# Batch 0 in high and low parts: weights decoded by ScalarE and an integer add, norms by reciprocal root

## The chip, the cores and the metric

The kernel runs on one core of a Trainium2 chip. The metric is device time in microseconds (us), the median of several runs; smaller is better. TensorE is the matrix engine (PE in the rows, PEld its weight loads), VectorE the elementwise engine (DVE), ScalarE the activation engine (ACT), GpSimd (POOL) and SyncE (SP) issue transfers.

## The reference

A linear attention (batch 8, 8 heads, 576 rows, 64 per head), normed per head, feeds a gated layer with a product over the rows:

```python
kv  = einsum('bhsd,bhse->bhde', k, v);  out = einsum('bhsd,bhde->bhse', q, kv)
x   = out / sqrt(mean(out*out, -1) + 1e-6) * g_norm          # then heads side by side: (8, 576, 512)
h   = maximum(x @ w_in, 0);  u, v = h[..., :512], h[..., 512:]
v_n = (v - mean(v)) / sqrt(var(v) + 1e-6)
v_s = einsum('ts,bsd->btd', w_spatial, v_n) + b_spatial[None, :, None]
return (u * v_s) @ w_out
```

All inputs are float32, and the host hands the two weight matrices over as int64 words, the pairs of which are float32 bits of two neighbouring columns seen as one double; the kernel decodes them.

## The kernel before, in words

**Numbers in two parts.** From batch 1 on every large product is made of three: a float32 number is cut in a high part (a cast to the matrix engine's rounded type `F32R`) and a low part (the rest), and high x high, high x low and low x high are summed in the accumulator (`hl`, L319; `three`, L313). A cut is a pair: ScalarE casts the high part, VectorE subtracts it from the number (`split`, L353 and L354; `split_w`, L727 and L728; `split_x`, L258 and L259). Batch 0 is made otherwise: its products take plain float32 (`hv_32`, L404; `hv_tail_32`, L410; `u_32`, L428; `sp_32`, L437 and L438), so that the first products need no cut. Its operands lie in `X32`, `W32`, `V32`, `VT32`. The weights are cut later, for batch 1, by `split_in` (token X) and `split_ws` (token E).

**Decoding.** A tile of 128 rows of a weight matrix (512 KB as int64 words) is decoded by one ScalarE step (`weight64_a`, L713) and five VectorE steps (`weight64_b`, L719 to L723). There are 12 such tiles, 8 of `w_in` in the first 45 us, 4 of `w_out` up to batch 1.

**Norms.** A reciprocal root (`rsqrt_a`, `rsqrt_b`) is a square root on ScalarE (L199) beside a product and a reciprocal on VectorE (L200, L201), and three small VectorE steps that correct it (L206 to L208). One is made for each pair of heads and each 128 rows of `v`.

**Order.** For batch 0 the string `PLAN` (L35) is a list of tokens: W and L start loads, c and C decode a weight, J and K make K^T V, A and D the attention rows and their squares, B their norm, T the transpose and the copy of `x`, H the product for v (chunk c, part k), e, F relu and norm of v, u the product for u, h the tail rows, s a spatial product with the gate. For batches 1 to 7 the strings `SEVEN`, `GATED`, `FIRST`, `EVEN`, `ODD` order the seven products of each 2x2 scheme, the steps of the next batch's attention and the output products. What the tokens emit is then put in order on each engine by the framework's scheduler, within the brackets and bars of the plan in program order. Engines run their queues in order.

**Memory.** `vpool` holds two tiles of 14 x 256 columns: for batch 0 they are `X32`, `W32`, `VT32`, from batch 1 on `VH` and `VL`. `WSH`, `WSL` hold seven quadrants of the cut spatial weights, `ps_mm` four accumulator banks, which H, u and s use in turn.

Of the kernel before, what the change touches and what calls it, by code (L numbers as in the profile page):

```python
# [8 lines left out]
F32 = mybir.dt.float32  # L9
# [37 lines left out]
p11 p61 p10 p20 p60 p21 p50 p70 p40 p51 p71 p41 p30 p31  # L47
# [3 lines left out]
p50 p10 p60 p70 p11 p20 p61 p40 p21 p30 p51 p71 p41 p31  # L51
# [3 lines left out]
p p p s p s s s s p p s p p p w s p p p s p p o o s o s o s s w s o s  # L55
# [3 lines left out]
s v v v s v s u y s s u s u u u u s u u s u u s s u u s u u s p p p s s s s p s s p p p p s p p s p  # L59
p s s p p s o o o o s s  # L60
# [3 lines left out]
v v v v u u u u u u s u s u u u u u u s u p p s s p p p p p s p p s s p s p p s s s s s p p o s o s  # L64
o o s o
# [8 lines left out]
def body(ctx: ExitStack, tc, qT, kvm, kvt, g2, w_in, wsT, bsp, w_out, out):  # L74
# [34 lines left out]
    VH = VL = None  # L109
    R = [vpool.tile([P, 14 * HF], F32, name=f"R{x}", tag=f"V{x}") for x in "HL"]  # L110
    X32 = R[0][:, 0:NP * XC].rearrange("p (k t) -> p k t", t=XC)
    VT32 = R[0][:, NP * XC:NP * XC + FH]
    W32 = [R[1][:, n * FH:(n + 1) * FH] for n in range(7)] + [R[0][:, NP * XC + FH:]]
# [82 lines left out]
    def rsqrt_a(ss, n, rows, mul, tag):  # L196
        a, s0, q, r = (small.tile([P, n], F32, name=f"{x}{tag}", tag=f"{x}{tag}")[0:rows]
                       for x in "asqr")
# [3 lines left out]
        return s0, q, r  # L202
# [58 lines left out]
    def att_t(b, p, st):  # L261
        x = st[p]
        ps = ps_att.tile([P, 512], F32, name="pstr", tag="att")
        for c in range(NC):
            nc.tensor.transpose(ps[:, c * P:(c + 1) * P], x[:, c * P:(c + 1) * P], ident)  # L265
        if b == 0:
            nc.scalar.activation(X32[:, p, 0:NT], ps, AF.Copy, scale=gcol)
        else:
            split_x(ps, XH[:, p, 0:NT], XL[:, p, 0:NT])

    def att_tail(b, st):
# [6 lines left out]
        if b < 2:  # L278
            nc.scalar.activation(X32[:, :, cols], v, AF.Copy, scale=gcol)
            cols = slice(TAILC[0], TAILC[0] + TAIL)  # L280
        if b == 0:
            return
        split_x(v, XH[:, :, cols], XL[:, :, cols])
# [101 lines left out]
    def hv_tail():  # L385
# [3 lines left out]
                   hl(XH[:, k, cols], XL[:, k, cols], WVH[:, k], WVL[:, k])])  # L389
# [13 lines left out]
    def hv_32(c, k):  # L403
        nc.tensor.matmul(psv[c], X32[:, k, c * P:(c + 1) * P], W32[k], start=k == 0,  # L404
                         stop=k == NP - 1)

    def hv_tail_32():
# [632 lines left out]
```

## Time and profile before

| | |
|---|---|
| median of 3 runs | 513.22 us (512.23 to 513.38) |
| span of the profiled execution | 511.2 us |
| around the span, median less span | 2.0 us |
| TensorE / its weight loads | 498.9 us (98%) / 438.4 us (86%) |
| VectorE | 408.8 us (80%) |
| ScalarE | 292.8 us (57%) |
| matrix instructions | 3436 |
| transfers | 72.22 MB, mean 141 GB/s |
| table loads on ScalarE | 1, of 1.283 us |

A profile is one execution. Its own time is known by its span alone, from the first to the last instruction; what the timed runs have beyond it lies around the program. A float32 product appears as two matrix instructions in a row, a product of high or low parts as one. Matrix instructions overlap, so one's duration is not what it costs in a row of them: a row's length by its count is.

### The profile page before, as it was taken

To read this page: it belongs to the slowest core of one execution; us is meant where nothing else is said; L and a number is where in the kernel's file an instruction comes from. 1 tells how busy PE (TensorE), PEld (TensorE's weight loads), DVE (VectorE), ACT (ScalarE), POOL (GpSimd) and SP (SyncE) were. 2 spreads that over 40 slices of the span, in tenths; PEclk is the share of its full clock that TensorE was granted. 3 is DMA by queue.
4 is the path that set the end of the run, shared out by engine and by line. 5 is a ranking of instruction groups with operands and counts; after the bars stand their busy time and mean duration, and the time that the engine had idled before them with its cause. 6 is when DMAs were issued, how large, how long until landed. Compare 5 with 4: busy or idle time off the path is not lost.

```text
span 511.2 us, 9846 instructions
## 1 busy us (share of the span) xinstructions
PE 498.9 (98%) x3436; PEld 438.4 (86%) x3436; DVE 408.8 (80%) x1193; ACT 292.8 (57%) x1000; POOL 28.7 (6%) x58
## 2 busy tenths in 40 slices
PE   6999999999999999999999999999999999999996
PEld 6758788898888899989998899988998889988995
DVE  3898599688997889778795689878898589987870
ACT  2555456896734796456641689347742579536421
POOL 5000000000010300010000100010000100010000
PEclk9999999999999999999999999999999999999999
DMA  7995300635354435354426615324444512315213
GB/s 256 311 347 193 103 23 2 238 90 174 123 193 137 129 126 207 117 170 138 133 93 228 203 41 194 112 78 176 135 165 144 171 30 63 131 42 165 91 76 103
DMA packets 28293, 72.22 MB, mean 141 GB/s; under 512 B 3602, under 2 KB 8210, under 8 KB 26708
## 3 DMA queue, kind: packets, MB, share of 16 engines
q1 hardware_dynamic: 23412, 48.01, 28.6%
q0 software_dynamic: 4832, 23.60, 13.9%
q8 instruction: 27, 0.44, 0.4%
q14 instruction: 22, 0.18, 0.1%
HBM read 58.48 MB, written 13.11 MB: 140 GB/s over the span
## 4 chain that ended last, share of the span: by engine, by line
PE 78%; DVE 8%; ACT 7%; DMA 5%; issue 1%; SPq 0%; ACTq 0%; DVEq 0%
PE pso L317 15%; PE psh L350 12%; PE psb L566 7%; PE pso L237 4%; PE psc L566 4%; PE psa L566 4%; PE psub L566 4%; PE pskv L162 4%; PE psu L428 3%; PE psa L437 3%; PE psua L566 3%; PE psh L404 3%; PE psuc L566 2%; PE pstr L265 2%; DMA KV<-kvm 2%; ACT x L220 2%
## 5 line engine op out<-in xcount | busy, mean ns | idle before, releaser
L317 PE MATMUL pso<-WO,G 128*128 128x512 f32 x384 | 94.4, 397 | 0.0
L317 PEld LDWEIGHTS pso<-WO,G 128*128 128x128 f32 x384 | 70.6, 188 | 14.5
L353 ACT CAST G<-SUMg 128x288 fp32r<-128x288 f32 (+1 forms) x56 | 22.8, 406 | 44.6 <-DVE SUMg L588 44.4
L220 ACT ACTIVATE x<-pso 128x64 f32<-128x64 f32 x208 | 44.8, 254 | 5.7 <-PE pso L237 5.5
L220 ACT ACTIVATION_READ_ACCUMULATOR x<-pso 128x1 f32 x208 | 43.9, 240 | 0.0
L350 PE MATMUL psh<-WVL,XH 128*128 128x512 f32 x112 | 43.9, 392 | 0.0
L350 PE MATMUL psh<-WVH,XH 128*128 128x512 f32 x112 | 43.8, 396 | 0.0
L350 PE MATMUL psh<-WVH,XL 128*128 128x512 f32 x112 | 43.3, 391 | 0.0
L668 ACT COPY o<-pso 128x512 f32<-128x512 f32 x35 | 20.2, 594 | 38.9 <-PE pso L317 28.7
L354 DVE TENSOR_TENSOR VL<-v,VH 128x512 fp32r<-128x512 f32 (+1 forms) x56 | 34.6, 620 | 2.7 <-ACT VH L353 2.2
L353 ACT CAST VH<-v 128x512 fp32r<-128x512 f32 (+1 forms) x56 | 31.7, 574 | 3.3 <-DVE v L382 2.1
L337 ACT ACTIVATE v<-v,mv,rv 128x512 f32<-128x512 f32 x28 | 23.5, 840 | 10.6 <-DVE mv L336 10.5
L354 DVE TENSOR_TENSOR G<-SUMg,G 128x288 fp32r<-128x288 f32 (+1 forms) x56 | 23.4, 417 | 7.2 <-ACT G L353 6.9
L258 ACT ACTIVATE XH<-pstr,gcol 128x512 fp32r<-128x512 f32 x28 | 19.4, 700 | 11.4 <-PE pstr L265 11.2
L566 PE MATMUL psb<-WSH,VH 128*128 128x288 f32 x84 | 25.6, 305 | 0.3 <-DVE U L549 0.2
L329 DVE BATCH_NORM_STATS2 s<-v 128x6 f32<-128x512 f32 x32 | 21.9, 689 | 4.5 <-ACT v L323 3.9
L350 PEld LDWEIGHTS psh<-WVH,XH 128*128 128x128 f32 x112 | 21.0, 188 | 4.6 <-ACT o L668 0.2
L350 PEld LDWEIGHTS psh<-WVL,XH 128*128 128x128 f32 x112 | 21.1, 188 | 4.4
L566 PE MATMUL psb<-WSL,VH 128*128 128x288 f32 x84 | 24.8, 295 | 0.0
L350 PEld LDWEIGHTS psh<-WVH,XL 128*128 128x128 f32 x112 | 21.0, 188 | 4.3
L162 PEld LDWEIGHTS pskv<-KV 128*64 128x64 f32 x512 | 18.1, 140 | 7.8 <-issue 3.9
L566 PE MATMUL psb<-WSH,VL 128*128 128x288 f32 x84 | 24.6, 295 | 0.0
(244 smaller groups left out, 1419.4 us busy)
## 6 DMA issues: line engine op xcount, KB each, us to landing
KV<-kvm SPq DMA_DIRECT2D x31, 512.0 KB, 5.0
WO<-spare_o POOLq DMA_DIRECT2D x12, 1024.0 KB, 7.0
UX<-spare_u POOLq DMA_DIRECT2D x18, 512.0 KB, 5.7
out<-o SPq DMA_DIRECT2D x32, 256.0 KB, 2.6
qt<-qT SPq DMA_DIRECT2D x16, 288.0 KB, 3.5
stage<-w_in SPq DMA_DIRECT2D x8, 512.0 KB, 6.5
qt<-qT SPq DMA_DIRECT2D x16, 256.0 KB, 2.7
KT<-kvt SPq DMA_DIRECT2D x32, 64.0 KB, 4.8
```

The lines of the kernel that those rows point to most:

```text
L162: return nc.tensor.matmul(ps[h:h + D, at:at + D], of[:, 0, h:h + D], of[:, 1, h:h + D], start=c == 0, stop=c == NC)
L220: nc.scalar.activation(x[:, cols], ps[0:rows, cols], AF.Square, accum_out=ss[:, h:h + 1])
L237: nc.tensor.matmul(ps[:, c * P:(c + 1) * P], qt[:, c * P:(c + 1) * P], st[p], start=True, stop=True)
L258: nc.scalar.activation(hi, ps, AF.Copy, scale=gcol)
L317: nc.tensor.matmul(ps, lt, rh, start=i == 0, stop=i == n - 1)
L329: nc.vector.bn_stats(s6, v)
L337: nc.scalar.activation(v, v, AF.Identity, bias=m, scale=r)
L350: nc.tensor.matmul(ps, lt, rh, start=k == 0 and i == 0, stop=k == NP - 1 and i == 2)
L353: nc.scalar.copy(hi, x)
L354: nc.vector.tensor_tensor(lo, x, f32(hi), op=ALU.subtract)
L566: nc.tensor.matmul(ps, lt, rh, start=start and i == 0, stop=stop and i == len(pairs) - 1, skip_group_check=True)
L668: nc.scalar.copy(o, ps)
```

## The change

Batch 0 no longer multiplies plain float32: x, v and the weights are cut before their first use and H, h, u and s are made of three products like those of the later batches. The cut x lies where batch 1's `VH`, `VL` will, the cut v in three quadrants of `WSH`, `WSL` that are filled later (`split_v`, token Y; `mix_ws`, token M, makes the four mixed quadrants, `split_ws` the four plain ones). A weight is decoded by two ScalarE steps and two VectorE steps, the second an integer add. A reciprocal root is one ScalarE step and three VectorE steps. All order strings are new.

```diff
@@ norms
-        a, s0, q, r = (small.tile(...) for x in "asqr")
-        nc.scalar.activation(s0, ss, AF.Sqrt, bias=epsc[0:rows], scale=mul)
-        nc.vector.tensor_scalar(a, ss, mul, EPS, op0=ALU.mult, op1=ALU.add)
-        nc.vector.reciprocal(q, a)
-    def rsqrt_b(s0, q, r):
-        nc.vector.tensor_tensor(r, s0, q, op=ALU.mult)
-        nc.vector.scalar_tensor_tensor(q, s0, -0.5, r, op0=ALU.mult, op1=ALU.mult)
-        nc.vector.scalar_tensor_tensor(r, q, 1.5, r, op0=ALU.add, op1=ALU.mult)
+        nc.scalar.activation(y, ss, AF.Abs_reciprocal_sqrt, bias=epsc[0:rows], scale=mul)
+    def rsqrt_b(ss, y, r, mul):
+        nc.vector.scalar_tensor_tensor(r, y, -0.5 * mul, y, op0=ALU.mult, op1=ALU.mult)
+        nc.vector.scalar_tensor_tensor(r, ss, EPS / mul, r, op0=ALU.add, op1=ALU.mult)
+        nc.vector.scalar_tensor_tensor(r, r, 1.5, y, op0=ALU.add, op1=ALU.mult)
@@ decoding
-        nc.scalar.activation(f32(t), f32(w1), AF.Abs, scale=2.0 ** -112)
+        low = staged[i][:, 0:DM]
+        nc.scalar.activation(f32(t), f32(wide[:, :, 1]), AF.Prelu, scale=2.0 ** -112, alpha=-2.0 ** 32)
+        nc.scalar.activation(low, wide[:, :, 0], AF.Copy, scale=2.0 ** -29)
         nc.vector.tensor_scalar(t, t, 3, None, op0=ALU.logical_shift_left)
-        nc.vector.scalar_tensor_tensor(w1, w1, 0x80000000, t, op0=ALU.bitwise_and, op1=ALU.bitwise_or)
-        nc.vector.tensor_scalar(t, w1, 0xFF800000, None, op0=ALU.bitwise_and)
-        nc.vector.scalar_tensor_tensor(f32(w0), w0, 2.0 ** -52, f32(t), op0=ALU.mult, op1=ALU.mult)
-        nc.vector.tensor_tensor(to, f32(w1), f32(w0), op=ALU.add)
+        nc.vector.tensor_tensor(low, t, low, op=ALU.add)
@@ x of batch 0
-        if b == 0:
-            nc.scalar.activation(X32[:, p, 0:NT], ps, AF.Copy, scale=gcol)
-        else:
-            split_x(ps, XH[:, p, 0:NT], XL[:, p, 0:NT])
+        hi, lo = (X0H, X0L) if b == 0 else (XH, XL)
+        split_x(ps, hi[:, p, 0:NT], lo[:, p, 0:NT])
@@ products of batch 0 (H and h take hv_k and hv_tail with X0H, X0L)
-            nc.tensor.matmul(psu[d], W32[NP + k][:, d * P:(d + 1) * P], X32[:, k, cols], ...)
+            multiply(psu[d], hl(WUH[:, k % 2, n, fs], WUL[:, k % 2, n, fs],
+                                X0H[:, k, cols], X0L[:, k, cols]), k == 0, k == NP - 1)
+    def split_v(c):
+        split_w(V0H[c], V0L[c], V32[:, c])
+    def sp_first(d, j):
+        multiply(ps, [m for c in range(NC) for m in
+                      hl(V0H[c][:, ds], V0L[c][:, ds],
+                         *(w[:, c % 2, (0, 6, 1, 2)[c // 2 * 2 + j]] for w in (WSH, WSL)))],
+                 True, False)
+        tail_product(ps, 0, d, j)
@@ orders, one line of each of six tables
-[ W N8 G L c W C J00 L A00 L c L C n6 W J01 A01 J02 B00 T00 W A02 c H00 H20 J03 B01 T01 H30 B02 D03
+[ N8 W L L c W J00 A00 B00 W J01 C X0 A01 L G n6 T00 J02 c C L A02 W B01 J03 H30 B02 c W H20 X1 L
-p50 p10 p60 p70 p11 p20 p61 p40 p21 p30 p51 p71 p41 p31
+p50 p10 p60 p11 p70 p61 p51 p20 p40 p21 p30 p71 p41 p31
```

Three places of the orders follow. The first is VectorE at the start of the program, from the first decoded weight (`stage`, `t`) to the first norm of attention rows (`ss`, `rh`, `x`). Before:

```order
L719 TENSOR_SCALAR t<-t 128x512
L720 SCALAR_TENSOR_TENSOR stage<-stage,t 128x512
L721 TENSOR_SCALAR t<-stage 128x512
L722 SCALAR_TENSOR_TENSOR stage<-stage,t 128x512
L723 TENSOR_TENSOR RL<-stage 128x512
L224 TENSOR_REDUCE ss<-x 128x8
```

and with the change:

```order
L704 TENSOR_SCALAR t<-t 128x512
L705 ISA stage<-t,stage 128x1024
L221 TENSOR_REDUCE ss<-x 128x8
L203 SCALAR_TENSOR_TENSOR rh<-yh 128x8
L204 SCALAR_TENSOR_TENSOR rh<-ss,rh 128x8
L205 SCALAR_TENSOR_TENSOR rh<-rh,yh 128x8
L226 TENSOR_TENSOR x<-pso,rh 128x512
L710 TENSOR_TENSOR WVL<-stage,WVH 128x512
```

Five decoding steps became two, the second of which the program holds as one instruction over 1024 16-bit elements per row, and the weight's low part (L710) now follows within batch 0's start.

The second place is TensorE where batch 0's spatial products (`psa`) begin, behind the tail rows (`psh`). Before:

```order
L428 MATMUL psu<-RH 128x288 x4
L275 MATMUL pstt<-ident,x 128x128 x4
L237 MATMUL pso<-KVO_103,qt 128x128 x4
L410 MATMUL psh<-RL,RH 128x512 x4
L437 MATMUL psa<-stage,V_127 128x288 x8
L265 MATMUL pstr<-ident,x 128x128 x4
```

and with the change:

```order
L312 MATMUL psh<-WVH,VH 128x512
L312 MATMUL psh<-WVL,VH 128x512
L312 MATMUL psh<-WVH,VL 128x512
L262 MATMUL pstr<-ident,x 128x128 x8
L551 MATMUL psa<-WSH 128x288
L551 MATMUL psa<-WSL,WSH 128x288
```

Eight transposes (`pstr`) of batch 1 were moved ahead of the spatial products, and these now read cut quadrants, among which the cut v lies (`WSH`, `WSL`), where they read the staged weights and `V32` as they were.

The third place is ScalarE at the same point: the rows around the relu of the tail rows (`v<-psh`). Before:

```order
L323 ACTIVATE v<-psh 128x512
L199 ACTIVATE sv<-mv,epsc 128x1
L223 ACTIVATE x<-pso 128x512
L258 ACTIVATE XH<-pstr,gcol 128x512
L727 CAST WSH<-stage 128x288 x3
L413 COPY RH<-v 64x512
```

and with the change:

```order
L770 CAST WTH<-WT_128 64x576
L772 CAST WTH<-WT_128 64x576
L774 CAST WTL_87<-WT_128 1x576 x2
L318 ACTIVATE v<-psh 128x512
L220 ACTIVATE x<-pso 128x512
L255 ACTIVATE XH<-pstr,gcol 128x512
L709 CAST WSH<-V_127 128x512
```

The last row is the high part of v's first chunk, which the first spatial products read; the casts of the tail weights (`WTH`, `WTL`) stand ahead of it, and the casts of spatial weights, which stood behind this point, are ahead of these.

## Rows read from the trace of the kernel before

**Rows 1.** The page: each engine's busy time in the span, and TensorE's busy tenths in 40 slices of it.

```profile
PE 498.9 (98%) x3436; PEld 438.4 (86%) x3436; DVE 408.8 (80%) x1193; ACT 292.8 (57%) x1000; POOL 28.7 (6%) x58
PE   6999999999999999999999999999999999999996
```

**Rows 2.** The whole span's waits of TensorE, by who ended them: us in total, times, longest us. The longest four.

```profile
PE pskv L162 <- DMA KV<-kvm: 2.4, 1, 2.4
PE pso L237 <- ACT KVB L180: 1.7, 3, 0.6
PE psw L825 <- DVE epsc L812: 1.1, 1, 1.1
PE psa L566 <- ACT SUMp L615: 0.5, 1, 0.5
```

**Rows 3.** The chain of work that ended last, in order of time, pieces of it: start us, us, what, and how many instructions.

```profile
17.96 0.22 ACT KVB L180
...
19.60 1.72 PE psh L404 x4
...
25.05 6.01 PE psh L404 x14
...
39.05 7.76 PE psu L428 x32
...
59.79 3.70 PE psh L410 x8
63.49 3.88 PE psa L437 x16
...
71.69 1.94 PE psa L438 x8
...
85.12 8.25 PE psh L350 x36
...
140.89 1.59 PE psb L566 x12
142.49 0.13 PE psb L572
...
493.46 13.75 PE pso L317 x60
```

**Rows 4.** Busy time by stretch: us, then PE, PEld, DVE, ACT, POOL busy us (and instructions), TensorE's granted clock, DMA share, GB/s.

```profile
30.00:40.00 10.00, 10.00 (x72) 6.00 (x71) 10.00 (x23) 6.22 (x13) 0.00 (x0) 1.00 1.01 327
17.00:64.00 47.00, 46.31 (x287) 31.79 (x284) 36.99 (x114) 25.27 (x84) 0.00 (x0) 1.00 0.71 233
64.00:130.00 66.00, 65.55 (x424) 55.84 (x424) 57.21 (x168) 48.67 (x171) 0.00 (x0) 1.00 0.31 102
```

**Rows 5.** VectorE's groups of instructions from 0 to 120 us: line engine op names shapes xcount | busy us, mean ns of one | idle before us.

```profile
L720 DVE SCALAR_TENSOR_TENSOR stage<-stage,t 128x512 uint32<-128x512 uint32 x12 | 8.0, 686 | 0.0
L722 DVE SCALAR_TENSOR_TENSOR stage<-stage,t 128x512 f32<-128x512 uint32 x11 | 7.4, 685 | 0.1
L728 DVE TENSOR_TENSOR WSL<-stage,WSH 128x288 fp32r<-128x288 f32 x14 | 5.9, 452 | 0.1
L719 DVE TENSOR_SCALAR t<-t 128x512 uint32<-128x512 uint32 x12 | 4.8, 421 | 5.9 <-ACT t L713 5.9
L721 DVE TENSOR_SCALAR t<-stage 128x512 uint32<-128x512 uint32 x11 | 4.7, 454 | 0.0
L723 DVE TENSOR_TENSOR RL<-stage 128x512 f32<-128x512 f32 x7 | 4.6, 686 | 0.1
L259 DVE SCALAR_TENSOR_TENSOR XL<-pstr,gcol,XH 128x512 fp32r<-128x512 f32 x5 | 3.7, 746 | 0.3 <-ACT XH L258 0.3
L201 DVE RECIPROCAL qh<-ah 128x8 f32<-128x8 f32 x12 | 2.4, 200 | 0.2
L207 DVE SCALAR_TENSOR_TENSOR qh<-sh,rh 128x8 f32<-128x8 f32 x12 | 1.8, 163 | 0.2
```

**Rows 6.** ScalarE's groups from 0 to 120 us, same columns.

```profile
L713 ACT ACTIVATE t<-stage 128x512 f32<-128x512 f32 x12 | 7.7, 668 | 7.9 <-DVE stage L722 3.1 <-DMA stage<-w_in 2.5 <-DMA stage<-w_out 2.3
L220 ACT ACTIVATE x<-pso 128x64 f32<-128x64 f32 x32 | 6.9, 256 | 1.2 <-PE pso L237 1.1
L727 ACT CAST WSH<-stage 128x288 fp32r<-128x288 f32 x14 | 5.6, 437 | 7.6 <-DVE stage L765 3.7 <-DVE stage L763 3.4 <-DVE stage L760 0.3
L199 ACT ACTIVATE sh<-ss,epsc 128x8 f32<-128x8 f32 x12 | 3.9, 329 | 4.9 <-DVE ss L224 4.8
L223 ACT ACTIVATE x<-pso 128x512 f32<-128x512 f32 x6 | 3.6, 596 | 5.0 <-PE pso L237 4.0 <-PE pstr L265 0.9
L258 ACT ACTIVATE XH<-pstr,gcol 128x512 fp32r<-128x512 f32 x5 | 3.4, 709 | 0.5 <-PE pstr L265 0.5
L431 ACT ACTIVATE U<-psu 128x288 f32<-128x288 f32 x8 | 3.3, 411 | 1.7 <-PE psu L428 1.3
L727 ACT CAST WVH<-RL 128x512 fp32r<-128x512 f32 x4 | 2.5, 631 | 0.0
L918 ACT ACTIVATE V<-psh 128x512 f32<-128x512 f32 x4 | 2.4, 592 | 0.7 <-PE psh L404 0.7
L785 ACT CAST WTL<-WT 1x576 fp32r<-1x576 f32 x2 | 1.3, 672 | 0.0
L279 ACT ACTIVATE RH<-pstt,gcol 128x256 f32<-128x256 f32 x2 | 0.9, 472 | 0.0
```

More of the change, by code (lines that the diff above doesn't have):

```diff
@@ L108, in body @@
     vpool = ctx.enter_context(tc.tile_pool(name="vpool", bufs=1))
[L109 to L113, printed above, removed]
+    VH, VL = (vpool.tile([P, 2, 7, HF], F32R, name=f"V{x}", tag=f"V{x}") for x in "HL")
+    flat = [x.rearrange("p k n f -> p (k n f)") for x in (VH, VL)]
+    X0H, X0L = (x[:, 0:NP * XC].rearrange("p (k t) -> p k t", t=XC) for x in flat)
+    V0H = [x[:, k, 3:6].rearrange("p n t -> p (n t)")[:, 0:FH] for x in (WSH, WSL) for k in range(2)]
+    V0L = [x[:, NP * XC + n * FH:NP * XC + (n + 1) * FH] for x in flat for n in range(2)]
     TA = [persistent([P, FH + HF], F32R, f"TA{i}") for i in range(2)]
@@ L277, in att_tail @@
         v = ps.rearrange("q (p t) -> q p t", t=P)[:, :, P - TAIL:P]
[L278 to L283, printed above, removed]
+        hi, lo = (X0H, X0L) if b < 2 else (XH, XL)
+        split_x(v, hi[:, :, cols], lo[:, :, cols])
+        if b == 1:
+            own = slice(TAILC[0], TAILC[0] + TAIL)
+            nc.scalar.copy(XH[:, :, own], f32(hi[:, :, cols]))
+            nc.scalar.copy(XL[:, :, own], f32(lo[:, :, cols]))
     def move_tail():
@@ L401, in hv_tail, with u_first @@
                 nc.vector.tensor_tensor(TA[i][other, cols], x[own], f32(hi), op=ALU.subtract)
[L403 to L407, printed above, removed]
-        ps = ps_mm.tile([P, 512], F32, name="psh", tag="mm")
-        for k in range(NP):
-            nc.tensor.matmul(ps, X32[:, k, NT:XC], W32[k], start=k == 0, stop=k == NP - 1)
-        v = work.tile([P, FH], F32, name="v", tag="v", bufs=3)
-        layer_norm(ps, v, nc.vector)
-        nc.scalar.copy(VT32[0:TAIL], v[0:TAIL])
-        own, other = slice(TAIL, P), slice(0, TAIL)
-        d = SUM["g"][:, 0, 0:HF]
-        nc.vector.tensor_tensor(d[own], v[own, 0:HF], v[own, HF:FH], op=ALU.subtract)
-        for x, cols in (v, slice(0, FH)), (d, slice(FH, FH + HF)):
-            hi = TA[1][own, cols]
-            nc.scalar.copy(hi, x[own])
-            nc.scalar.copy(TB[1][own, cols], x[own])
-            nc.vector.tensor_tensor(TA[1][other, cols], x[own], f32(hi), op=ALU.subtract)
-    def u_32(j, k):
+    def u_first(j, k):
         cols = slice(j * HS, (j + 1) * HS)
@@ L730, in split_in @@
     def split_in(n):
+        x = decoded.pop(n)
         if n < NP:
-            split_w(WVH[:, n], WVL[:, n], W32[n])
+            split_w(WVH[:, n], WVL[:, n], x)
         else:
@@ L740, in make_out @@
         weight64_a(2 * NP + k)
-        decoded[k] = weight64_b(2 * NP + k)
+        weight64_b(2 * NP + k)
         if pin:
@@ L745, in split_out, with quadrants, mix_ws @@
     def split_out(k):
[L746 removed]
+        split(WO[:, 0, k], WO[:, 1, k], decoded.pop(2 * NP + k))
         for i in range(2):
             nc.sync.dma_start(spare_o[:, i, k], f32(WO[:, i, k]))
+    def quadrants(k):
+        t, t2 = staged["s", k], staged["s", k + 2]
+        return t[:, 0:HS], t[:, HS:S], t2[:, 0:HS], t2[:, HS:S], t[:, S:S + HS], t2[:, S:S + HS]
     def split_ws(k):
[L752 to L754 removed]
+        b11, b12, b21, b22, _, _ = quadrants(k)
+        for n, of in (0, b11), (6, b12), (1, b21), (2, b22):
+            split_w(WSH[:, k, n], WSL[:, k, n], of)
+    def mix_ws(k):
+        b11, b12, b21, b22, x, y = quadrants(k)
         def keep(n, of):
@@ L812, in body @@
     nc.vector.memset(epsc, EPS)
-    nc.scalar.activation(small.tile([P, 1], F32, name="warm", tag="av"), epsc, AF.Sqrt)
+    nc.scalar.activation(small.tile([P, 1], F32, name="warm", tag="yv"), epsc, AF.Abs_reciprocal_sqrt)
     nc.gpsimd.memset(KVB[:, 0], 0.0)
@@ L935, in body @@
     ahead(len(todo))
-    VH, VL = (vpool.tile([P, 2, 7, HF], F32R, name=f"V{x}", tag=f"V{x}") for x in "HL")
     def first():
```

68 lines of the change are left out of this document (28 added, 40 removed).

## The prediction

> **What bounds the kernel now.** I read the page first: TensorE is busy 98% of the span and in 39 of 40 slices nearly without a gap, VectorE 80%, ScalarE 57% [rows 1]. Busy matrix time can hide gaps, so I went to TensorE's waits: the three longest groups, 5.2 us together, all belong to the first 20 us (the first keys and values, the first copies of K^T V, the warm-up), and the next one in size is 0.5 us in the whole span [rows 2]. So from 19.6 us, where the first product for v starts [rows 3], to 507.2 us, where the last output product ends, TensorE does not wait, and a microsecond of its work is a microsecond of the kernel. The chain of waits says the same: from there to 95 us it runs over matrix rows almost alone, and its pieces give what a product costs when they stand in a row [rows 3]. The table of stretches shows who feeds it: from 17 to 64 us VectorE is busy 37.0 of 47 us and ScalarE 25.3, from 64 to 130 us 57.2 and 48.7 of 66 [rows 4]. The granted clock is 1.00, the upper of its two levels (2.4 GHz).
>
> **TensorE's work, step by step.** All from pieces of the chain [rows 3].
> - A float32 product over 512 columns is two instructions: 14 took 6.01 us, 0.859 each product. Three products of parts: 36 took 8.25 us, 0.2292 each, 0.688 for three. H has 16 such products, h 4 (there 8 instructions took 3.70 us; I use 0.859 again). 20 x (0.859 - 0.688) = 3.4 us less.
> - Over 288 columns float32 costs 7.76 / 16 = 0.485 us, and three parts 1.59 / 4 = 0.398. u has 32 products: 2.8 us less.
> - The spatial products are 32 more at 0.485 (16 instructions in 3.88): 2.8 us less. Their 8 tail products go from 0.485 (8 instructions in 1.94) to two parts of 0.13 each (L572; L574 is alike): 8 x 0.22 = 1.8 us less.
>
> Together 10.8 us, and all of it on the path. Nothing is added on TensorE. Of the moved rows, the eight transposes that now stand ahead of the spatial products only change places.
>
> **What feeds it.** VectorE loses per decoded weight five steps (L719 to L723: 0.40, 0.67, 0.43, 0.67 and 0.66 us, busy time by count, together 2.83) and keeps a shift (0.40) and an add [rows 5]. The trace has no integer add. Its nearest rows are the two-operand steps over the same bytes, 0.67 us (L720); the order holds it as 1024 elements of 16 bits where those are 512 of 32, so at one element a beat it would be about twice as long, 1.34. I take 0.67, the row with the same bytes, and keep 1.34 for the range. Saved: 2.83 - 1.07 = 1.76 us a weight, 21 us over 12. A reciprocal root loses a product and a reciprocal (L201, 0.20) and keeps three steps like L207 (0.15): about 0.35 us, worth nothing on a VectorE that nobody waits for after 130 us.
>
> As to that add, the Trainium skill's "VectorE: DVE Perf Modes", section on the perf-mode tier table, says that a two-operand step goes at one element a cycle in fp32 and at two where all operands are 16 bits wide. By that rule it takes the 0.67; read as a step without that faster program it takes the 1.34, and the time would be that of the third rival below. No row here shows which.
>
> What is added lies in batch 0's start. ScalarE gets a second step per weight, which I price as the first (L713, 7.7 us for 12, 0.64), since it reads the same strided words; and both engines get, ahead of the spatial products, the cuts that stood behind them or were not there: weights, x, v, spatial quadrants. To see whether they keep up I sum each engine's rows in the new order, from the copies of the third K^T V (from 17.7 us now, the second of the pair being at 17.96 [rows 3]) to the high part of v's first chunk, which the first spatial product reads.
> - ScalarE [rows 6]: 18 decoding steps at 0.64 (11.5 us); 10 casts of 512 at 0.62 (6.2); 8 of 288 at 0.40 (3.2); 4 copies of x at 0.68 (2.7) and 4 of its tails at 0.45 (1.8); 7 squares and the tail's relu at 0.60 and 4 relus of v at 0.60 (6.6); one accumulating square, 8 x 0.22 (1.7); 8 relus of u at 0.41 (3.3); 4 casts of tail weights at 0.65 (2.6); 8 K^T V copies and 10 roots at 0.32 (5.9). Sum 45.5, so it is there at 63.2 us.
> - VectorE [rows 5]: 40 long steps (adds, low parts, reductions, norms, statistics) at 0.67 (26.8), 4 low parts of x at 0.74 (3.0), 9 shifts at 0.40 (3.6), 8 low parts of 288 at 0.42 (3.4), 37 small ones at 0.16 (5.9). Sum 42.7, there at 60.4 us.
> - TensorE begins its spatial products at 63.49 us now [rows 3]. The order before them saves 3.4 + 2.8 = 6.2 us and gets the 0.9 us of the eight transposes ahead (about 0.11 each): 58.2 us.
>
> So TensorE comes first. From ScalarE's sum it waits 5.0 us. Steps that stand close behind each other overlap: the 32 squares of L220 with their 32 accumulator reads fill 6.9 us where L220's means alone add to 8.2 [rows 6]; with an eighth off, the sum ends at 57.5 us and the wait is nothing. Against that, neither engine can be busy all the time while it waits for the other: as many as 2 us more, 7 in all. I take 3.6, the middle of 0 and 7, for no row is nearer to either end.
>
> Behind that point the cover holds: ScalarE's rows to the next high part of v are about 4.5 us, beside 36 products (4.8 us) and an attention row of TensorE. From there to 130 us VectorE has lost three decodings and 8 long cuts, and ScalarE has taken cuts ahead that stood there. The start to 19.6 us I leave as it is: weights 1 and 2 are loaded behind the second K, V and Q instead of between, the fourth K, V ahead; bounds 1 us either way. On the same queue two spatial tiles now stand behind batch 1's third K, V, which waits for its buffer; their cuts come late in ScalarE's order, behind the relus of v, which covers it, and without that cover they are late by one landing. The end (the last 60 output products from 493.46 us, then the copies and stores) is the same [rows 3].
>
> **Sum.** 513.2 - 10.8 + 3.6 = **506.0 us**. The span of 511.2 would become 504.0; the 2.0 us around it stay.
>
> **The rivals.**
> 1. *TensorE is fed all along.* 513.2 - 10.8 = 502.4 us. For it: ScalarE's 21.7 idle us, and that VectorE ran full from 30 to 40 us without stopping TensorE [rows 4]. Against it: two sums that end behind 58.2 us.
> 2. *ScalarE is late by its whole sum.* Its steps don't overlap, and it waits for VectorE besides: 7.0 us, 509.4. For it: each second decoding step waits for the first, whose tile it writes over, so these pairs cannot overlap. Against it: the idle time just named. The Trainium skill's "ScalarE: Activation LUTs", section on rules for kernel authors, speaks against the trade in this way: cheap elementwise work belongs on VectorE, which does it faster. By that rule the decoding moved to the wrong engine and this rival is the result; the rows of the two engines (0.64 us a step against 0.40 to 0.67) neither bear it out nor refute it.
> 3. *The integer add takes a beat for each 16-bit half.* 9 adds in the stretch cost 0.67 us more each: VectorE is there at 66.4 us, TensorE waits 8.2 less the 8 products (1.1 us) that need no low part: 7.1, so 509.5 us.
> 4. *The new tables for batches 1 to 7 cost waits.* TensorE has hardly any there, so they can only lose; a first gate that comes 0.5 us late in each batch (the longest such wait now [rows 2]) adds 3.5 us to the forecast: 509.5 us.
> 5. *Slower: ScalarE's copy of whole words is dear.* It reads and writes 32-bit integers, which no row does on this engine. Place: the nine copies ahead of the first spatial product. It decides from the point where the wait passes 10.8 us, that is 5.8 us over ScalarE's sum, 0.64 us a copy: at 1.28 us, twice the row, the gain is gone. At three times, 1.92 us, the wait is 5.0 + 11.5 = 16.5 and the time 518.9 us. Against it: L713 reads words at the same stride and takes little more than a plain activation of that size (0.668 against 0.596 us for L223 [rows 6]).
>
> That the change does not do what it says can be excluded: the order shows the products by three, two steps for five, and one table load as before.
>
> **How the numbers follow.** Chances: forecast 0.40 (its own range, wait 1 to 6 us, 503.4 to 508.4), the rivals in order 0.20, 0.14, 0.10, 0.10 and 0.06. The range reaches from the first rival less the start's 1 us to rivals two, three and four with 1 us more: 501.5 to 510.5 us; outside lie the fifth and the tails of the others, some 0.15. About 0.2% (1 us) is what a measurement can tell from no change. Faster by more: all but the fifth and a tenth of rivals two to four, 0.90. Within it: 0.04, from those tails. Slower: 0.06.
>
> **What would show it.** In the changed profile three products over 512 columns should take 0.69 us and 288 columns 0.40; batch 0's spatial products should start near 62 us, with TensorE's wait there ended by ScalarE's or VectorE's part of v; the integer add's mean should be near 0.69 us, ScalarE's two decoding steps near 0.67 each; ScalarE should be busy over 40 of the 47 us from 17 to 64; and batch 1's first product for v, now at 85.12 us [rows 3], should start near 79, a K^T V product of batch 2 (1.3 us) having moved ahead of it. If it starts there and the time is still above 508, the later tables are the cause. Waits of TensorE over 8 us between 20 and 80 us would prove the forecast wrong, and so would a time above 510.5.

## The result, and the profile after

The change takes 505.9 us (median of 6 runs, 502.96 to 506.6) against 512.9 (511.85 to 516.31): a ratio of 0.984, 95% interval 0.981 to 0.988, 7 us less. Run again later it took 505.7, ratio 0.986 (0.983 to 0.989). The profiled execution is the second fastest of the first six, 503.1 us with a span of 501.3 and a granted clock of 1.000; four of the six had a mean clock of 0.988 or 0.989 and took 505.7 to 506.6 us, so the profile is read for its stages and not for the median.

The page's rows of TensorE's busy time, which answer to [rows 1]:

```profile
PE 487.3 (97%) x3520; PEld 442.2 (88%) x3520; DVE 383.4 (76%) x1020; ACT 298.9 (60%) x992; POOL 28.0 (6%) x57
...
PE   6999899999999999999999999999999999999996
```

TensorE has 11.6 us less busy time, VectorE 25, and ScalarE 6 more; one slice, the fifth (50 to 63 us), is no longer full. TensorE's longest waits (us in total, times, longest), the answer to [rows 2]:

```profile
PE pskv L162 <- DMA KV<-kvm: 2.7, 4, 1.9
PE psa L551 <- ACT WSH L709: 1.9, 1, 1.9
PE pso L234 <- ACT KVB L180: 1.7, 3, 0.6
PE psw L814 <- DVE epsc L801: 1.1, 1, 1.1
PE psh L345 <- ACT o L653: 0.6, 1, 0.6
PE psh L345 <- DVE WVL L710: 0.5, 1, 0.5
```

The second row is new: the first spatial product waits for ScalarE's cast of v's first chunk. The last but one stands at the end of batch 1. Pieces of the chain of waits, which answer to [rows 3]:

```profile
28.39 2.11 PE psh L345 x8
...
33.96 5.62 DMA KV<-kvm
39.58 0.04 issue
39.62 0.80 PE pskv L162 x20
...
44.09 6.36 PE psu L551 x48
...
59.07 0.58 ACT v L318
...
60.16 0.69 ACT XH L255
60.85 0.51 ACT WSH L709
61.41 1.33 PE psa L551 x8
...
78.48 1.59 PE psa L551 x12
80.33 10.92 PE psh L345 x48
```

Three parts over 512 columns take 10.92 / 16 = 0.682 us, over 288 columns 1.59 / 4 = 0.398 us, as priced. The chain leaves TensorE twice. At 39.6 us a K^T V product of batch 1, which the order puts among the first products of u, has waited for its keys and values (0.2 us). And from 59.07 us the chain runs over ScalarE. By this trace the cast at its end is late by its place in ScalarE's queue: VectorE's last norm of v ran from 49.23 to 49.77 us, but ScalarE then had the last relus of u, four casts of tail weights (56.30 to 59.02 us), the tail's relu, a square and a cast of x to do ahead of it, without a pause from 55.5 us on. No run here moves that cast. The stretches of [rows 4] and the decoding rows of [rows 5] and [rows 6]:

```profile
17.00:64.00 47.00, 43.54 (x371) 38.75 (x365) 40.44 (x103) 41.12 (x106) 0.00 (x0) 1.00 0.70 225
20.00:39.00 19.00, 18.24 (x150) 14.87 (x146) 16.28 (x39) 17.08 (x48) 0.00 (x0) 1.00 0.97 320
64.00:130.00 66.00, 65.69 (x494) 60.79 (x493) 51.77 (x139) 45.82 (x152) 0.00 (x0) 1.00 0.38 122
```

```profile
L705 DVE CUSTOM_DVE_ANT_0 stage<-t,stage 128x1024 uint16<-128x1024 uint16 x12 | 8.2, 683 | 0.6 <-ACT stage L699 0.3
L704 DVE TENSOR_SCALAR t<-t 128x512 uint32<-128x512 uint32 x12 | 5.2, 435 | 5.1 <-ACT t L698 5.1
```

```profile
L699 ACT ACTIVATE stage<-stage 128x512 uint32<-128x512 uint32 x12 | 8.3, 688 | 0.2
L698 ACT ACTIVATE t<-stage 128x512 f32<-128x512 f32 x12 | 8.2, 686 | 2.9 <-DMA stage<-w_in 2.6 <-DMA stage<-w_out 0.3
```

From 17 to 64 us ScalarE is busy 41.1 of 47 us (25.3 before) and VectorE 40.4 (37.0): batch 0 now keeps three engines nearly full. Up to 39 us the DMA engines are as full (a share of 0.97), as they were before.

**Where the time went, by stage.** One profile each; the start of the first product of a stage, in us, read from TensorE's timeline. "Rest" is from batch 1's first product for v to the last matrix product.

| kernel | v | u | spatial | batch 1's v | rest |
|---|---|---|---|---|---|
| before | 19.4 | 38.9 | 63.3 | 84.7 | 422.1 |
| the change | 20.0 | 39.0 | 61.4 | 80.2 | 416.3 |
| e1 again | 22.7 | 41.7 | 63.9 | 82.7 | 416.5 |
| e2 v in two parts | 20.1 | 38.6 | 62.2 | 80.4 | 427.9 |
| e3 ScalarE step twice | 22.2 | 43.2 | 71.6 | 91.2 | 416.1 |
| e4 old tables | 22.9 | 41.9 | 64.0 | 82.8 | 421.7 |
| e5 longer warm-up | 22.6 | 42.0 | 63.6 | 83.7 | 419.3 |
| e6 before, new decoding | 19.5 | 38.4 | 63.8 | 85.3 | 426.4 |
| e7 no second ScalarE step | 19.9 | 37.2 | 61.9 | 80.4 | 426.1 |
| e8 old decoding | 20.0 | 45.1 | 73.7 | 95.4 | 419.9 |
| e9 warm-up, early g | 20.6 | 39.3 | 61.9 | 80.7 | 419.8 |
| e10 before, new tables | 19.3 | 38.8 | 63.2 | 84.6 | 426.1 |
| e11 e7, own buffer | 22.0 | 39.3 | 63.1 | 81.3 | 421.5 |
| e12 own buffer | 19.9 | 38.9 | 61.1 | 79.8 | 417.7 |

Counting each stage's products at their prices gives its work, an estimate. From the first product for v to batch 1's it was 64.5 us of work in 65.3 before, and is 54.7 in 60.2: 4.6 us more lost to waits. In the rest it was 412.1 in 422.1 and is 410.3 in 416.3: 4.0 us fewer lost. So the span's 9.9 us are 10.8 of work less and 4.0 won later, with 4.6 given back in batch 0 and 0.3 at the ends. In e1, where the clock was low at the start, 2.65 us more went there. "Lost" is what a stage takes beyond that work; it holds the waits, stretches at the lower clock, and gaps too short for the rows of waits.

### The profile page after: what moved, and what is told of

Read it like the earlier page. It is cut to its first block, busy times and chain, and to the rows that moved or that the text cites. A ratio compares the mean times of both kernels' runs of the same rounds, so it can differ in the third digit from the quotient of the medians.

```text
span 501.3 us, 9753 instructions
## 1 busy us (share of the span) xinstructions
PE 487.3 (97%) x3520; PEld 442.2 (88%) x3520; DVE 383.4 (76%) x1020; ACT 298.9 (60%) x992; POOL 28.0 (6%) x57
## 4 chain that ended last, share of the span: by engine, by line
PE 80%; DVE 6%; ACT 6%; DMA 6%; issue 1%; SPq 0%; DVEq 0%; ACTq 0%
PE pso L312 17%; PE psh L345 14%; PE psb L551 6%; PE psa L551 6%; PE pso L234 5%; PE psub L551 4%; PE psc L551 4%; PE pskv L162 4%; DMA KV<-kvm 4%; PE psua L551 3%; PE psuc L551 3%; PE psu L551 3%; PE psu L312 3%; PE pstr L262 2%; PE psh L312 2%; DMA out<-o 1%
## 5 line engine op out<-in xcount | busy, mean ns | idle before, releaser
L348 ACT CAST G<-SUMg 128x288 fp32r<-128x288 f32 (+1 forms) x56 | 22.6, 407 | 49.7 <-DVE SUMg L573 49.4
L217 ACT ACTIVATE x<-pso 128x64 f32<-128x64 f32 x200 | 42.6, 253 | 10.1 <-PE pso L234 10.0
L653 ACT COPY o<-pso 128x512 f32<-128x512 f32 x35 | 20.1, 591 | 41.5 <-PE pso L312 35.4
L217 ACT ACTIVATION_READ_ACCUMULATOR x<-pso 128x1 f32 x200 | 41.8, 239 | 0.0
L162 PE MATMUL pskv<-KV 128*64 128x64 f32 x512 | 21.8, 232 | 2.7 <-DMA KV<-kvm 2.7
```

The costliest lines, as they stand in the source:

```text
L162: return nc.tensor.matmul(ps[h:h + D, at:at + D], of[:, 0, h:h + D], of[:, 1, h:h + D], start=c == 0, stop=c == NC)
L217: nc.scalar.activation(x[:, cols], ps[0:rows, cols], AF.Square, accum_out=ss[:, h:h + 1])
L348: nc.scalar.copy(hi, x)
L653: nc.scalar.copy(o, ps)
```

## The experiments

Theory: batch 0 is now paced by ScalarE and VectorE, which hand on part of what TensorE saves; the rest came from the later rows. Rivals: TensorE's own work sets the time as before, or the tables matter nothing. Two further rivals were not tested by a run of their own, and the traces below speak for both: that the order of ScalarE's queue, and not the sum of its work, sets the wait; and that the transfers of the first 40 us do. One thing bears on every total: the planner (the framework's scheduler) lays out the rows behind the start anew whenever an edit changes what it reckons with, so batch 0's stages are compared by the table above and the totals with care.

**e1: the change again.** No edit.

> The changed kernel once more, unaltered. Its six runs so far lie on two levels, 503.0 to 503.1 us at a mean granted clock of 1.000 and 505.7 to 506.6 at 0.988. A mean of 0.988 over 504 us is what some 12 us at the lower level (half of the upper) would give. Theory A: the low stretch lies before 20 us, where TensorE waits for the first keys and values; then the windows of a run at 0.988 show a clock near 0.5 there for about 12 us and 1.00 behind 20 us, and everything behind comes about 3 us later. Rival B: it lies at the new wait of 1.9 us at 59.5 us; then the clock is below 1.00 in the stretch from 60 to 75 us. Rival C: it has no fixed place. Time 503.0 or 506.1 by level.

Measured: 505.7 us (504.47 to 508.05), profile with a clock of 0.990. Stretches of it (the column behind the five engines is the granted clock):

```profile
5.00:10.00 5.00, 2.03 (x23) 1.64 (x24) 1.30 (x2) 1.61 (x4) 2.54 (x5) 0.88 1.05 326
10.00:15.00 5.00, 4.47 (x36) 4.07 (x35) 2.48 (x6) 1.93 (x5) 0.00 (x0) 0.50 1.03 370
15.00:20.00 5.00, 5.00 (x41) 4.68 (x40) 1.88 (x5) 1.57 (x3) 0.00 (x0) 0.60 1.05 266
20.00:25.00 5.00, 4.41 (x46) 3.89 (x45) 3.63 (x8) 3.97 (x11) 0.00 (x0) 1.00 1.01 360
```

and the same twelve filler instructions on TensorE's timeline (start us, us), in e1 and then in the change's first profile:

```profile
15.80 2.77 PE L837 MATMUL psh<-KVB 128*128 128x128 f32 x12
```

```profile
14.70 1.50 PE L837 MATMUL psh<-KVB 128*128 128x128 f32 x12
```

The clock is at its lower level (1.2 GHz) from about 9 to 19 us and never behind it; the first product for v starts 2.65 us later, and everything behind keeps that distance. Theory A on the place is right. What its text made of levels is not: here the times do not sort by clock (506.7 us at 1.000, 504.5 to 505.6 at 0.998), so the clock is one part of the scatter and not all of it.

**e2: less TensorE work ahead of the spatial products.**

```diff
-        for i, (lt, rh) in enumerate(pairs):
+        for i, (lt, rh) in enumerate(pairs[:parts]):
```

The rest of the edit hands `parts` = 2 to batch 0's H.

> Batch 0's product for v leaves out the third part (low x of high weights): 16 products of 0.229 us, 3.7 us less work on TensorE between 20 and 56 us; ScalarE and VectorE keep all of theirs. Theory A (the forecast): the first spatial product waits for ScalarE's cast of v, so the time that TensorE saves ahead of it turns into a longer wait there; the wait of 1.9 us at 59.5 us grows to about 5, and the time falls by 0 to 1 us against the unaltered change. Rival B: TensorE's own work sets the pace there and the wait is a chance of the order; the time falls by 3 to 3.7 us.

Measured: batch 1's first product at 80.4 us against 80.2. Not a microsecond of the 3.7 came through: u starts 0.4 us sooner, the spatial products not sooner at all. (One K^T V product of 1.3 us moved behind that point, which makes it plainer still.) So rival B's 3 us did not come, but theory A's picture is not what the trace shows either: the wait for the cast of v did not grow, it is gone. Three other waits of TensorE, and a stretch at the lower clock, took the time:

```profile
27.48 0.50 PE L345 MATMUL psh<-WVH,VH 128*128 128x512 f32 x1 [1.73 <-ACT WVH L709]
...
40.07 0.69 PE L162 MATMUL pskv<-KV 128*64 128x64 f32 x16 [0.78 <-DMA KV<-kvm]
...
61.81 0.63 PE L262 MATMUL pstr<-ident,x 128*128 128x128 f32 x4 [2.58 <-DVE x L226]
```

```profile
30.00:35.00 5.00, 5.00 (x53) 3.90 (x52) 4.83 (x12) 3.84 (x9) 0.00 (x0) 0.73 0.52 176
```

In the change these waits are 0.3, 0.2 and none, with 1.9 for the cast. The clock was at its lower level for some 3.4 us from 29.3 us on, which took about 1.7 us of TensorE's saving (an estimate: half of the stretch). So the run shows that what TensorE saves ahead of u is lost again, in part to ScalarE, in part to transfers and the clock. The kernel took 515.1 us, 9 more, and that lies in the rest, where the planner moved rows:

```profile
PE psh L345 <- ACT o L653: 5.7, 1, 5.7
```

These 5.7 us stand at the end of batch 1, where the change waits 0.6; behind them the clock was at its lower level from 162 to 169 us.

**e3: more ScalarE work.** The first decoding step issued twice.

> ScalarE's first decoding step is issued twice for each of the 12 weights: 0.69 us more each, 9 of them (6.2 us) ahead of the first spatial product. Theory A (ScalarE's sum sets the wait at 59.5 us): the first spatial product comes 4 to 6 us later, the wait grows from 1.9 to 6 or 8 us, and the kernel is 4 to 6 us slower than the unaltered change. Rival B (ScalarE has room, as its idle 6 us between 17 and 64 us say, and the wait came from VectorE or from TensorE's own results): 0 to 1.5 us slower.

Measured: 513.2 us, 7.5 more than e1; from the first product for v to the spatial ones 49.4 us against 41.3. Theory A's direction, above its upper end: the waits moved to u, whose weights came late, and the clock fell behind them (lower level from 52 to 59 us), which alone costs up to 3 us of the 8 (an estimate: half of that stretch, less its wait). ScalarE has no room for 6 us more; that does not yet say that its work sets the time without them (e7).

```profile
PE psu L551 <- ACT WUH L710: 4.2, 1, 4.2
...
PE psh L345 <- ACT o L653: 1.6, 1, 1.6
PE psa L551 <- DVE U L424: 1.2, 1, 1.2
```

**e4: the five later tables as they were.** `SEVEN`, `GATED`, `FIRST`, `EVEN` and `ODD` of the kernel before.

> The change with the old five tables for batches 1 to 7; only batch 0's order stays new. In the profile of the change TensorE waits about 1.5 to 2 us less between 95 and 507 us than before. Theory A: the new tables took these waits away; with the old ones they are back, and the time is 1 to 2 us longer than the unaltered change. Rival B: they went with VectorE's shorter roots, or are a matter of the single profile; the time stays within 0.5 us.

Measured: 508.5 us (507.07 to 511.22) against e1's 505.7; batch 0 the same to 0.1 us; the rest 421.7 against 416.5. Behind the new batch 0 the new tables are worth 3 us by the medians and 5 by the profiles: theory A, more than it said.

**e5: a longer warm-up.** `N8` became `N8 N5`.

> Thirteen warm-up products at the start instead of eight, so that TensorE has work until about 7.2 us instead of 4.9 (0.47 us each at the speed that the warm-up shows); the second half of the first keys and values lands at 7.6 to 7.8 us in any case. Behind the first 40 us the planner lays out some rows anew. Theory A (the idle 2 us ahead of the first keys are what lets the clock stay low until 19 us in some runs): the clock is 1.00 from 12 us on in nearly all runs, the first product for v starts at 20.0 us or earlier, and the time is 503 us in most runs, 2.5 us less than the unaltered change. Rival B (the time at which the clock rises has nothing to do with that wait): the first product for v at 22.7 us as often as before, the time 505.7, or 1 us more for the later first keys.

Measured: 509.1 us. The clock did rise early (eight products of the first attention row in 1.16 us from 9.1 us, where e1 and the change took 2.07 and 2.08), but the first product for v came at 22.6: TensorE then waited 1.4 us for the third keys and 1.5 for ScalarE, which stood until g had landed at 18.0 us, and the clock was at its lower level from 19 to 22 us. Neither theory's time; it showed what comes next.

**e6: the kernel before with the new decoding and roots.** Old products, old tables.

> The kernel before with the change's decoding (two steps on ScalarE, a shift and an integer add on VectorE) and its norms by reciprocal root, and nothing else: TensorE's products and the tables of the order stay (the planner lays out the later rows anew). VectorE has some 21 us of decoding and 15 us of roots less, ScalarE 8 us more. Theory A (the forecast: TensorE's work is the time, VectorE is not): 512.9 us give or take 1, at most the waits of about 2 us behind 95 us less. Rival B (VectorE, full from 30 to 45 us and from 60 to 80 us, has been holding TensorE back in ways that its waits do not show): 4 us or more less.

Measured: 517.7 us against 512.5, slower. Batch 1's first product at 85.3 against 84.7: VectorE's 18 us less work up to 85 us (46.8 busy against 65.2) bought nothing in batch 0, as theory A says. Most of the 5 us more are in the rest (426.4 against 422.1), which neither theory foresaw; TensorE waits there 1.9 us for keys and values and 1.0 for a relu of v, which it did not before.

**e7: ScalarE's second step taken away.**

```diff
-        nc.scalar.activation(low, wide[:, :, 0], AF.Copy, scale=2.0 ** -29)
-        nc.vector.tensor_tensor(low, t, low, op=ALU.add)
+        nc.vector.scalar_tensor_tensor(low, w0, 29, t, op0=ALU.logical_shift_right, op1=ALU.bitwise_or)
```

> The change without ScalarE's second decoding step: VectorE's integer add becomes one step that shifts the low word right by 29 and joins it to the shifted high word (bitwise or). The low three bits are cut off instead of rounded. ScalarE has 12 x 0.69 us less, 9 of them (6.2 us) ahead of the first spatial product; VectorE's step is of the same size, about 0.67 us. Theory A (ScalarE's chain sets the waits in batch 0): the first spatial product starts 2 to 4 us sooner than with the unaltered change (61.4 us where the first product for v starts at 20.0), so does batch 1's first product for v (80.2 there), and its wait of 1.9 us for ScalarE's cast is gone; the time 2 to 3 us less if the later rows, which the planner lays out anew, keep their pace. Rival B (those waits are not ScalarE's): within 1 us at these places.

Measured: from the first product for v to u 17.3 us against 19.0, so ScalarE had set the pace there; but to the spatial products 42.1 against 41.4. The wait for ScalarE's cast is gone, and two others of TensorE have taken its place, for a transfer and for a norm of VectorE (the first two rows; then ScalarE and VectorE ahead of that norm):

```profile
40.27 0.69 PE L162 MATMUL pskv<-KV 128*64 128x64 f32 x16 [1.11 <-DMA KV<-kvm]
...
61.55 0.63 PE L262 MATMUL pstr<-ident,x 128*128 128x128 f32 x4 [2.38 <-DVE x L226]
```

```profile
57.92 1.36 ACT L773 CAST WTL<-WT 1x576 fp32r<-1x576 f32 x2
59.31 0.30 ACT L198 ACTIVATE yh<-ss,epsc 128x8 f32<-128x8 f32 x1
```

```profile
59.64 0.17 DVE L203 SCALAR_TENSOR_TENSOR rh<-yh 128x8 f32<-128x8 f32 x1 [3.05 <-ACT yh L198]
```

What was won up to u went first to batch 1's keys and values, which let the K^T V product start at 40.3 us here and at 39.6 in the change. The norm then came late not for VectorE's work: VectorE stood 3.05 us for a root that ScalarE makes, behind its casts of the tail weights. And ScalarE's cast of v, with 6 us of work taken away ahead of it, began at 61.0 us, in the change at 60.8. (In e2 the norm waits in the same way, 3.05 us.) So the places stay within 1 us, as rival B says, though ScalarE is still in the chain: it is not the sum of its work that sets the start of the spatial products. The order of its queue behind the last products of u, and the transfer ahead of them, account for it in these traces; no run varies either alone. The total, 513.5 us, is again the rest's (426.1), with the same 5.7 us for `psh` at the end of batch 1 as in e2.

**e8: the old decoding.** One ScalarE step and five VectorE steps a weight; the rest of the change kept.

> The change with the old decoding: one step on ScalarE and five on VectorE (0.40, 0.67, 0.43, 0.67, 0.66 us) for each weight; products by three parts, roots and tables stay as in the change. VectorE gets 9 x 1.76 = 15.8 us more ahead of the first spatial product, ScalarE 6.2 less. Theory A (batch 0's cuts keep both engines full, so the new decoding is what lets TensorE have its shorter products): the first spatial product 8 to 14 us later than 61.4 us, waits of TensorE ended by VectorE's low parts, and a time of 513 to 520 us, the gain over before gone. Rival B (VectorE has room): within 3 us of the change.

Measured: 522.5 us, ratio to the kernel before 1.020 (1.017 to 1.023), 17 more than the change. The spatial products start at 73.7 us, 12.3 later.

```profile
PE psu L551 <- ACT WUH L711: 8.2, 1, 8.2
...
PE psa L551 <- ACT WSL L711: 2.8, 1, 2.8
PE psh L345 <- ACT WVH L711: 2.4, 1, 2.4
```

Theory A, in the place, and a little over its time: without the new decoding the shorter products cost more than they save, and by e6 neither half gains alone. The waits' rows name ScalarE's casts, which read what VectorE decodes (VectorE busy 49.5 us of the 53.7 from the first product for v on). Not all of the 12.3 us is VectorE's: the clock was at its lower level around 30 to 36 and 54 to 60 us, worth some 4 to 5 us (an estimate: half of the time that TensorE worked there), and ScalarE stood 3.5 us for a transfer of an output weight at 52.5 us.

```profile
30.00:35.00 5.00, 4.18 (x12) 3.22 (x12) 5.00 (x11) 0.55 (x1) 0.00 (x0) 0.50 0.63 221
```

**e9: the longer warm-up with g loaded early.** `[ N8 N5 W L G L`, and `G` taken out further on.

> The change with thirteen warm-up products instead of eight, as in the longer warm-up alone, and the load of g (0.5 KB) issued eight loads sooner, behind the first keys, values and queries: with the longer warm-up alone ScalarE waited 2.9 us for it. The tail of the spatial weights stands one key-value load sooner, as there; every other row of the five engines stands as in the unaltered change but for two neighbours. Theory A (the clock rises early when TensorE does not stand idle ahead of the first keys, and what remained was ScalarE's wait for g): full speed from 9 us on, the first product for v at 19 to 20 us in the profile, a time of 501 to 503.5 us in most runs, 2 to 4 us less than the 505.7 of the unaltered change on its own chip. Rival B (the third keys and values and the clock decide whatever the start does): first product for v at 22 us or later, 505 to 507 us.

Measured: 506.7 us (505.87 to 511.03), first product for v at 20.6 us. TensorE's timeline (the bracket: idle before, and who ended it):

```profile
8.41 1.16 PE L234 MATMUL pso<-KVB,qt 128*128 128x128 f32 x8 [0.58 <-ACT KVB L180]
...
16.65 0.69 PE L162 MATMUL pskv<-KV 128*64 128x64 f32 x16 [1.45 <-DMA KV<-kvm]
...
18.47 1.13 PE L234 MATMUL pso<-KVB,qt 128*128 128x128 f32 x8 [1.00 <-DMA qt<-qT]
...
20.56 0.50 PE L345 MATMUL psh<-WVH,VH 128*128 128x512 f32 x1
```

Full speed from 8.4 us on, and no gain: the transfers bind the start at some 20 us. Theory A's time is refuted, and rival B's place too. The rest took 419.8 us, 3.5 more than in the change's profile with the same order of rows but for two neighbours. The rows of waits name most of it: 1.5 us more at the end of batch 1, in the row below, and 1.2 more for keys and values (1.6 against 0.4 behind 86 us).

```profile
PE psh L345 <- ACT o L653: 2.1, 1, 2.1
```

Such a difference between two nearly equal programs is as large as the effects of the tables; two profiles of the change itself (the first and e1) differ by 0.2 us in the rest.

**e10: the kernel before with the new tables.**

> The kernel before with the change's five tables for batches 1 to 7 and nothing else; batch 0 stays to the row. From batch 1's first product for v (84.7 us before) to the last matrix product it takes 422.1 us before, 416.3 in the change, 421.7 in the change with the old tables. Theory A (the new tables are the better ones, whatever stands in batch 0): this stretch takes 416 to 419 us and the kernel 509 us, 3 to 5 less than before. Rival B (the tables fit the change, with its shorter roots and its earlier start of batch 1, and nothing else): 421 us or more, and no gain or a loss.

Measured: 517.3 us against 513.2 (ratio 1.007, 1.004 to 1.010); the rest 426.1 against 422.1. Rival B: the same tables that win 3 to 5 us behind the change lose 4 behind the old batch 0.

**e11 and e12: the wait at the end of batch 1.** VectorE's cut of the summed weights (`w`, tag `stg`, two buffers) waits 3.4 us in the change until the store of an output has landed. In e7 it waits 6.4 us, for which the profile names no releaser; the runs' theory takes it for the same kind of store. ScalarE's next cast waits for it, the copies of outputs stand behind that cast, and TensorE waits for an accumulator. The cut in the change and in e7:

```profile
149.81 0.42 DVE L349 TENSOR_TENSOR w<-v,w 128x256 fp32r<-128x256 f32 x1 [3.40 <-DMA out<-o]
```

```profile
155.33 0.42 DVE L349 TENSOR_TENSOR w<-v,w 128x256 fp32r<-128x256 f32 x1 [6.43 <-issue]
```

The edit of both runs puts batch 1's output 2 under the tag `v` in place of `stg`; e11 has e7's edit besides.

```diff
-        if (b, c % 2) == (B - 1, 0):
+        if (b, c % 2) == (B - 1, 0) or (b, c) == (1, 2):
```

> The change without ScalarE's second decoding step, as before, and with batch 1's output 2 in a buffer of the tag of v (three of them) instead of the tag stg (two), which it shares with the cuts of the summed weights. Without that TensorE waited 5.7 us there at 157 us and its clock then fell to half for 7 us: VectorE's cut of the summed weights stood 6.4 us until the store of an output had left its buffer. Theory A (that one buffer costs it): this wait and the low clock behind it are gone, 6 to 9 us less than the 513.5 of that kernel, 505 to 507 us. Rival B (another output or the planner's new rows put a wait of the same size in its place): 511 us or more. Batch 1's first product for v at 80 us by both.

> The change with batch 1's output 2 in a buffer of the tag of v instead of stg, and nothing else; the planner lays out some 10% of the later rows anew. In the change VectorE's cut of the summed weights waits 3.4 us there for the store of an output, TensorE 0.6 us (2.1 in two other kernels with the same rows). Theory A: these waits go; 505.7 less 0.5 to 2 us, and fewer runs above 506. Rival B (the new layout costs as much elsewhere): 506 to 509 us.

Measured: e11 508.1 us, 5.4 less than e7; e12 505.5 (503.75 to 505.8) against e1's 505.7. The cut in e11 and in e12:

```profile
156.04 0.43 DVE L349 TENSOR_TENSOR w<-v,w 128x256 fp32r<-128x256 f32 x1 [6.11 <-issue]
```

```profile
150.08 0.42 DVE L349 TENSOR_TENSOR w<-v,w 128x256 fp32r<-128x256 f32 x1 [4.01 <-DMA out<-o]
```

VectorE waits as before, 6.1 and 4.0 us, so theory A of both is wrong as it was put. In e12 the row still names the store of an output, and the last one issued ahead of it (144.70 us) is batch 1's first, not the one I moved; in e11 it names none. e11 gained because an output's copy came to stand ahead in ScalarE's queue (157.15 us, directly behind the cast of `w`, where in e7 a square, a root and five casts come first, 160.98): TensorE waited 0.9 and 1.3 us in place of 5.7, and the clock did not fall behind it. In e12 TensorE's 0.6 us went and 1.1 us for a square of ScalarE's came elsewhere (`psuc <- ACT x`): the time is the change's, within what a median can tell, below rival B's range and above theory A's. None of these kernels is measurably faster than the change.

## Why the prediction was right, and where it was not

The time (506.0 us forecast, 505.9 measured) and the place of the wait were right, and the number owes its closeness to luck: the later batches won 4.0 us that the sum does not have, and against that stand 1.0 more in batch 0 and, in the four runs with the lower mean clock, nearly 3 us more, which by e1 go at the start.

- **TensorE's work, 10.8 us less:** right in size (0.682 and 0.398 us for three parts; busy time less by 11.6). "All of it on the path" failed: the stretch from v to u has some 1.9 us less work (an estimate by the prices) and is 0.4 us shorter, and in e2 3.7 us less work there moved nothing behind it. What TensorE saves there counts only as far as the other engines and the transfers let it; the prediction sums no transfers.
- **The wait ahead of the spatial products, 3.6 us:** right in place and near in size, not in its reason. They started at 61.4 us (61.8 by the sum), stopped by ScalarE, busy 41.1 of the 47 us. The wait itself is 1.9 us; short waits ahead of it make 1.0, and with the gaps batch 0 loses 4.6. From 17.7 to 61.4 us ScalarE was busy 39.4 us, the sum of 45.5 with an eighth off (39.8), and idle 4.4, where the prediction allowed 2; the middle of 0 and 7 was taken for want of a row and happened to be near. e3 shows that ScalarE has no room for more and e8 that VectorE has none; but e7 shows that less work for ScalarE brings its cast of v no sooner. Its place in the queue does, or the transfer ahead of u: that is argued from the traces and not shown by a run.
- **The integer add:** 0.683 us, the row with the same bytes; the third rival is refuted. 1024 elements of 16 bits took no longer than 512 of 32. The Trainium skill's "VectorE: DVE Perf Modes", section on the perf-mode tier table, gives a two-operand step twice the elements a cycle where all are 16 bits wide; the row agrees.
- **ScalarE's second step:** 0.688 us against 0.64 (the first is 0.686), 0.05 us a step more. The fifth rival, whole words dear, is refuted, and the second (509.4) as well: ScalarE's steps did overlap, and the spatial products started 3.8 us ahead of the 65.2 that its 7 us would give. The Trainium skill's "ScalarE: Activation LUTs", section on rules for kernel authors, would have such steps on VectorE; e7 took one off ScalarE and gained 1.7 us up to u and nothing at the spatial products, so no run here decides for the rule or against it.
- **Decoding and roots worth nothing in themselves:** right for batch 0 (e6). With the old decoding in the change, its roots kept, the kernel takes 17 us more (e8): VectorE's freed time is the cover that the cuts need. That the kernel before would become 5 us slower with them was not seen.
- **Batch 1's first product near 79 us:** 80.3, late by about what batch 0 lost beyond the forecast.
- **The later batches:** the step that failed. The sum has no term for the tables, and the fourth rival let them only lose, since TensorE has "hardly any" waits there. In fact the rest lost 10.0 us beyond its products' work before and loses 6.0 now (an error of the prices would stand in both). The rows of waits hold little of that, from 86 us on 2.4 us before and 1.3 now. What changed lies mostly in matrix instructions that start 0.15 to 0.5 us late: together 4.3 us before, 1.1 in the change, 1.2 in e1 and 3.9 with the old tables in e4 (an estimate: each start against the usual distance of its kind). So e4 puts 3 to 5 us of it to the tables, in this kernel; in the old one they lose 4 (e10), and why is open.
- **The start, "1 us either way":** right in the profile (0.6 us, one K^T V row more), wrong in the run of e1, where the lower clock to 19 us made it 3.2. In such runs this takes back most of what the tables give.

By the profile alone (503.1 us) the first rival, 502.4, would have been nearer. It is not what happened: TensorE was not fed all along in batch 0, and the later batches made up for it.

## What to carry to other kernels

When the bounding engine's work is cut, sum the rows of those that feed it, and the transfers, and then follow the order of their queues: here 10.8 us of matrix work went, and batch 0 handed 4.6 back. An engine that has no room for more work (e3) need not be the one whose work sets the time (e7). A decoding that was worth nothing on the old kernel was the condition for the new one, so parts of such a change are tried together and apart. Where an order is fitted to durations, every edit upstream refits it: the later rows of these kernels took 416 to 428 us for the same work to within 2 us, so read an edit's effect in its own stage before believing a total.

## What the runs showed that was not expected

- The first 11 us of TensorE are at half speed in the change's profile although its rows grant 1.00: eight instructions took 2.08 us at 9.19 us and 1.16 at 13.48. In e1 the row is at 0.50 from about 9 to 19 us and the same eight take 2.08 at 13.50 as well. With the warm-up running to 6.8 us instead of 4.9 (e9) they take 1.16 at 8.41.
- Long waits of TensorE were followed by a stretch at the lower clock: 4.2 and 1.0 us (e3) by 52 to 59 us, 5.7 us by 162 to 169 (e2) and 159 to 166 (e7). So were waits of 2.2 us (e5) and 2.6 (e11) ahead of the spatial products, by 3 us from 62 or 63 us on, one of 1.7 us in e2 (27.5 us), by 3 us from 29 us on, and one of 2.4 us in e8 (29.5 us), by 7 us. Waits ahead of the spatial products of 2.6 us in e2, 2.4 in e7 and 1.9 in the change were not. So the length of the wait alone does not tell.
- In the change a store of 256 KB held its buffer for 5.0 us (issued at 144.76 us, gone at 149.8), and three engines stood in line behind it: VectorE 3.4 us, ScalarE 5.2 behind VectorE, TensorE 0.6.
